# A spectral layer and two MLPs on one core: token chunks of 504 or 500 in place of 512 and a last 384

## The chip, the core and the metric

The kernel runs on one core of a Trainium2 chip. The metric is device time in microseconds (us) from the first to the last instruction; lower is better. Engines are named as the profile names them: PE multiplies matrices (PEld is its weight load), DVE, ACT and POOL work elementwise, SP issues the DMAs. TensorE has two clock levels, 1.2 and 2.4 GHz; the profile shows the granted one.

## What is computed

Cut to what matters, with B x S = 2 x 3008 = 6016 tokens of 256 features and 2048 hidden units:

```python
X = rfft(x, axis=1)
Y = soft_threshold(X @ (w_r + 1j * w_i) + b, 0.01)
y = irfft(Y, n=3008).reshape(6016, 256)
h = y @ w_in1
y = (h * sigmoid(h)) @ w_out1
h = y @ w_in2
out = np.maximum(0.01 * h, h) @ w_out2
```

All of it is in float32. The two MLPs (layer 1 and layer 2) are the part that the change touches.

## The kernel before, in words

**Numbers in two halves.** To keep float32 accuracy from single-pass matmuls, every operand is a rounded high part and a rest, the low part. A product is three matmuls: low weights by high data, high weights by low data, high by high (`product`, L574). ACT casts the high parts (`high`, L567), and DVE or POOL subtracts to get the low parts (`lower`, L530).

**Chunks and pairs.** Tokens run along the free axis. `CHUNKS` (L27) cuts the 6016 tokens into eleven chunks of 512 and a last one of 384. Each layer goes over the 12 chunks, and in each chunk over 8 pairs of hidden tiles of 128. A pair makes two tiles ph with `first` (L499): 6 matmuls for each, 12 in all, over the n tokens of the chunk. Then come the activation (`activate`, L509) and the products of the second matrix.

**Three modes of the second matrix** (L496). It has two hidden tiles by two output tiles in a pair.
- "plain" (layer 1, chunks 0 and 1): four products over n tokens, 12 matmuls.
- "blocks" (chunks of 512): the chunk is split into two halves of 256 tokens, and seven products over half a chunk do the work of eight, 21 matmuls. The seven need sums of hidden blocks: `t1` on POOL, `t23` and `t4` on DVE, into the tile u of six blocks. Their results stand in four accumulators and are put together at the end of the chunk in `finish` (L607).
- "tail" (the chunk of 384): four products over 384 tokens, 12 matmuls, with no `t1` and no `t4`, two accumulators, and a `finish` of two copies (L620 on ACT, L621 on DVE).

**The order of the work** is written out by hand: instructions stand on each engine as the last loop (from L656) issues them. One turn of the loop handles three pairs at once. The newest (`pr`) does `first` and `activate`; the one before (`one`) makes its sums, casts and subtractions; the one before that (`two`) multiplies. Between them `make_next` issues steps for the coming chunk:
- in layer 1 `inverse` (L402), which multiplies the inverse transform into px and splits it into the ring of x tiles (xhi by ACT, xlo by DVE, L416 and L417);
- in layer 2 `load_x2` and, in the turn of the last pair of a chunk, twice `split_x2` (L428), which casts xhi on ACT and subtracts xlo on POOL (L432).

In that last turn the two `split_x2` stand before and behind `pr.t1()` on POOL. The first `first` of the next chunk needs both.

**The ring** (L398) holds 3 x 512 tokens; a token's place is its number modulo 1536. `inverse` makes 376 or 188 tokens at a time, and cuts them only where the ring wraps.

**Weights.** In the last chunk of layer 1 the weights of layer 2 are made: `next_in` (L485 on ACT, L486 on DVE) from its second pair on, `sums_w2` on POOL (L462) and `split_w` (L468 on ACT, L469 on DVE) from its fourth and fifth pair on, and these go on into the first pairs of layer 2.

The functions that the change touches, with the line numbers of the profile:

Of the kernel before, what the change touches and what calls it, by code (L numbers as in the profile page):

```python
# [71 lines left out]
def spectral_mlp_kernel(ctx, tc, x, w_r, w_i, b_r, b_i, w_in1, w_out1, w_in2, w_out2, da, ea, dm, out):  # L72
# [325 lines left out]
    ring = [big.tile([128, 2, RING], F32R, name=f"x{p}") for p in parts]  # L398
    at = lambda t: t % RING
    accs, x2f, late = {}, {}, {}  # L400

    def inverse(h, c):  # L402
# [25 lines left out]
    def split_x2(c, h):  # L428
        t0, n = CHUNKS[c]
        hi, lo = (r[:, h, at(t0):at(t0) + n] for r in ring)  # L430
        nc.scalar.copy(hi, x2f[c][h])
        nc.gpsimd.tensor_tensor(out=lo, in0=x2f[c][h], in1=hi.bitcast(F32), op=ALU.subtract)  # L432
# [55 lines left out]
    class Pair:  # L488
# [51 lines left out]
        def t1(self):  # L540
            if self.mode == "blocks":
                blk = lambda k: self.u[:, k * 256:(k + 1) * 256]
                nc.gpsimd.tensor_tensor(out=blk(1), in0=blk(0), in1=blk(2), op=ALU.subtract)  # L543

        def t23(self):
            u, b2, n = self.u, self.ph[1], self.n
            if self.mode == "blocks":
                v = u.rearrange("p (j n) -> p j n", n=256)
                b22 = b2[:, :256].rearrange("p (j n) -> p j n", j=1).to_broadcast([128, 2, 256])
                nc.vector.tensor_tensor(out=v[:, 3:5], in0=b22, in1=v[:, 0:2], op=ALU.subtract)  # L550
            else:
                nc.vector.tensor_tensor(out=u[:, n:2 * n], in0=b2, in1=u[:, :n], op=ALU.subtract)

        def t4(self):
            u, b2 = self.u, self.ph[1]
            if self.mode == "blocks":
                nc.vector.tensor_tensor(out=u[:, 1280:], in0=u[:, 1024:1280], in1=b2[:, 256:], op=ALU.subtract)  # L557

        def parts(self, which):
            n = self.n  # L560
            if which == "1":
                return self.h1, self.l1, self.ph[1]
            if self.mode == "blocks":
                return (self.ha, self.la, self.u[:, 256:768]) if which == "a" else (self.hb, self.lb, self.u[:, 768:])
            return (self.ha[:, :n], self.la[:, :n], self.u[:, :n]) if which == "a" else (self.hb[:, :n], self.lb[:, :n], self.u[:, n:2 * n])
# [13 lines left out]
        def acc(self, i):  # L579
            key = self.layer, self.c, i  # L580
            if key not in accs:
                accs[key] = ps_a[i // 2].tile([128, 512], F32, tag="acc", name="acc")
            return accs[key]

        def products(self, which):
            if self.mode == "plain":
                s = "ab".index(which)
                f = 2 * self.p + s
                hi, lo = ((self.ha, self.la), (self.hb[:, :512], self.lb[:, :512]))[s]
# [6 lines left out]
            blk = lambda a, k: a[:, k * 256:(k + 1) * 256]  # L596
            if self.mode == "blocks":
# [4 lines left out]
            else:  # L602
                for i, w, b, e in {"1": [(0, A12, True, False)], "a": [(0, A11, False, True), (1, S1, True, False)],
                                   "b": [(1, A22, False, True)]}[which]:
                    self.product(self.acc(i)[:, :self.n], wh[w], wl[w], hi, lo, b, e)

        def finish(self, part):  # L607
            if self.p != NF // 2 - 1:
                return
            key, n = (self.layer, self.c), self.n  # L610
# [8 lines left out]
            if self.mode != "blocks":  # L619
                nc.scalar.copy(o[0], self.acc(0)[:, :n])  # L620
# [149 lines left out]
```

## Time and profile before

| what | value |
|---|---|
| median of 3 runs | 1210.31 us (1208.16 to 1210.81) |
| profiled execution, span (the only time it has) | 1212.1 us |
| PE busy | 1199.7 us, 99% |
| PEld busy | 1074.2 us, 89% |
| DVE, ACT, POOL busy | 843.5, 782.8, 567.2 us |
| mean granted clock of TensorE | 0.997 |

The profiled execution is one run of its own and is 1.8 us longer than the median of the others. Matmuls are pipelined, and their recorded lengths overlap: a 128x256 matmul is recorded with 0.28 us while the next one starts 0.12 us after it. So the price of a matmul is read as the distance from one start to the next, over many of them. In a timeline a row gives the start, the length, the engine, the line, and the operation with output and inputs; "x2" merges two neighbours, and brackets tell how long the engine was idle before it and what ended that.

### The profile page before, as it was taken

The page shows a single profiled execution, that of the slowest core. Times are in us where ns is not written, and L with a number is a line of the kernel's source. Part 1 is how long each engine was busy: PE and PEld are TensorE (multiplying, and loading weights), DVE is VectorE, ACT ScalarE, POOL GpSimd, SP SyncE. Part 2 cuts the span into 40 slices and gives each one's busy share as a digit, 9 for nine tenths or more (in the row PEclk, how much of TensorE's full clock was granted, in tenths as well). Part 3 has the DMA queues.
Part 4 walks back from the last instruction along what each step waited for, and adds up shares of the span by engine and source line. Part 5 has one row for each costly group of instructions (what it writes and reads, how often), then busy time and mean ns, then how long its engine had stood idle before and what let it go on. Part 6 is the DMA issues. An engine that isn't in the chain of part 4 may idle for free.

```text
span 1212.1 us, 20092 instructions
## 1 busy us (share of the span) xinstructions
PE 1199.7 (99%) x7346; PEld 1074.2 (89%) x7346; DVE 843.5 (70%) x1525; ACT 782.8 (65%) x1614; POOL 567.2 (47%) x606
## 2 busy tenths in 40 slices
PE   9899999999999999999999999999999999999998
PEld 9788888888999999989999988988888898888898
DVE  0588879768888988888888895555555455555543
ACT  3698977656666666666665776656656665665664
POOL 0233525544444444544545575555545455554532
PEclk9899999999999999999999999999999999999999
DMA  9344444001111111101100110111011011001000
GB/s 212 100 122 127 147 124 137 24 14 48 51 36 59 58 40 49 57 26 55 45 26 19 35 32 1 35 36 35 2 36 36 1 36 35 29 8 36 32 1 31
DMA packets 35883, 61.62 MB, mean 51 GB/s; under 512 B 3908, under 2 KB 15784, under 8 KB 35784
## 3 DMA queue, kind: packets, MB, share of 16 engines
q1 hardware_dynamic: 35784, 60.33, 16.3%
q8 instruction: 58, 0.95, 0.3%
q14 instruction: 41, 0.34, 0.1%
HBM read 41.70 MB, written 18.61 MB: 50 GB/s over the span
## 4 chain that ended last, share of the span: by engine, by line
PE 92%; DMA 2%; DVE 2%; ACT 1%; POOL 1%; issue 1%; SPq 0%; DVEq 0%; ACTq 0%; POOLq 0%
PE ph L506 43%; PE acc L576 39%; PE pz L310 5%; PE py L329 3%; DMA xt<-in_x_dram 2%; PE px L409 2%; PE pb L352 1%; DVE wm L128 1%; DVE zl L320 0%; ACT wm L125 0%; PE pa L255 0%; SPq L237 0%; DVE py L337 0%; POOL xlo L432 0%; DVE alo L302 0%
## 5 line engine op out<-in xcount | busy, mean ns | idle before, releaser
L531 POOL TENSOR_TENSOR la<-u,ha 128x512 fp32r<-128x512 f32 (+1 forms) x176 | 232.7, 1322 | 246.8 <-ACT ha L569 246.0
L531 DVE TENSOR_TENSOR lb<-u,hb 128x768 fp32r<-128x768 f32 (+1 forms) x176 | 178.2, 1013 | 220.7 <-ACT hb L569 219.0
L506 PE MATMUL ph<-xhi,winlo 128*128 128x512 f32 (+1 forms) x768 | 240.3, 394 | 0.5 <-DVE la L531 0.5
L506 PE MATMUL ph<-xlo,winhi 128*128 128x512 f32 (+1 forms) x768 | 239.1, 391 | 1.2 <-POOL xlo L432 1.2
L506 PE MATMUL ph<-xhi,winhi 128*128 128x512 f32 (+1 forms) x768 | 237.6, 391 | 0.0
L525 ACT ACTIVATE u<-ph 128x512 f32<-128x512 f32 (+1 forms) x192 | 113.7, 592 | 142.7 <-PE ph L506 142.6
L506 PEld LDWEIGHTS ph<-xlo,winhi 128*128 128x128 f32 x768 | 144.0, 188 | 36.3 <-POOL xlo L432 5.5
L506 PEld LDWEIGHTS ph<-xhi,winhi 128*128 128x128 f32 x768 | 143.8, 188 | 30.8
L543 POOL TENSOR_TENSOR u<-u 128x256 f32<-128x256 f32 x160 | 125.8, 786 | 65.2 <-DVE u L526 58.6
L569 ACT CAST hb<-u 128x768 fp32r<-128x768 f32 (+1 forms) x176 | 140.3, 797 | 9.4 <-DVE u L557 4.9
L576 PE MATMUL acc<-lb,whi 128*128 128x256 f32 (+1 forms) x496 | 141.1, 284 | 0.0
L576 PE MATMUL acc<-hb,whi 128*128 128x256 f32 (+1 forms) x496 | 139.6, 281 | 0.0
L576 PE MATMUL acc<-hb,wlo 128*128 128x256 f32 (+1 forms) x496 | 139.5, 281 | 0.0
L528 ACT ACTIVATE ph<-ph 128x512 f32<-128x512 f32 (+1 forms) x96 | 55.1, 574 | 113.2 <-PE ph L506 113.2
L506 PEld LDWEIGHTS ph<-xhi,winlo 128*128 128x128 f32 x768 | 120.5, 189 | 3.9 <-DVE la L531 1.0
L526 DVE SCALAR_TENSOR_TENSOR ph<-u,ph 128x512 f32<-128x512 f32 (+1 forms) x112 | 76.5, 683 | 65.1 <-ACT u L525 65.0
L569 ACT CAST ha<-u 128x512 fp32r<-128x512 f32 (+1 forms) x176 | 109.7, 623 | 14.7 <-POOL u L543 14.7
L531 DVE TENSOR_TENSOR l<-ph,h 128x512 fp32r<-128x512 f32 (+1 forms) x176 | 117.2, 666 | 0.0
L550 DVE TENSOR_TENSOR u<-ph,u 128x512 f32<-128x512 f32 x160 | 109.0, 681 | 6.3 <-POOL u L543 6.3
L569 ACT CAST h<-ph 128x512 fp32r<-128x512 f32 (+1 forms) x176 | 102.2, 581 | 2.6 <-DVE ph L526 1.5
L576 PE MATMUL acc<-ha,whi 128*128 128x256 f32 (+1 forms) x352 | 102.2, 290 | 0.0
L576 PE MATMUL acc<-la,whi 128*128 128x256 f32 (+1 forms) x352 | 100.9, 287 | 0.0
(123 smaller groups left out, 2675.8 us busy)
## 6 DMA issues: line engine op xcount, KB each, us to landing
wraw<-in_moe_w_in_dram SPq DMA_DIRECT2D x32, 256.0 KB
wraw<-in_moe_w_out_dram SPq DMA_DIRECT2D x32, 256.0 KB
scr<-bo SPq DMA_DIRECT2D x48, 128.0 KB
scr<-x2o SPq DMA_DIRECT2D x22, 256.0 KB
x2i<-scr SPq DMA_DIRECT2D x22, 256.0 KB
out_dram<-x2o SPq DMA_DIRECT2D x22, 256.0 KB
dmr<-in_dm_dram SPq DMA_DIRECT2D x34, 160.0 KB
bt<-scr SPq DMA_DIRECT2D x14, 384.0 KB
```

Of the source, the lines that this page charges most:

```text
L310: nc.tensor.matmul(pz, lhsT=u[:, h, :], rhs=v[:, h].rearrange("p g e -> p (g e)"), start=(n == 0), stop=(n == len(terms) - 1))
L329: nc.tensor.matmul(py, lhsT=u, rhs=v, start=(n == 0), stop=(n == len(terms)))
L409: nc.tensor.matmul(px[:, s * PAIR:(s + 1) * PAIR], lhsT=bt[:, s, h * 128:(h + 1) * 128], rhs=ea_sb, start=True, stop=True, skip_group_chec ...
L506: nc.tensor.matmul(ph, lhsT=u[:, h, f * 128:(f + 1) * 128], rhs=v[:, h, :], start=(i == 0), stop=(i == len(terms) - 1))
L525: nc.scalar.activation(out=th, in_=ph, func=ACTF.Tanh)
L526: nc.vector.scalar_tensor_tensor(out=out, in0=th, scalar=1.0, in1=ph, op0=ALU.add, op1=ALU.mult)
L528: nc.scalar.activation(out=out, in_=ph, func=ACTF.Prelu, alpha=0.01)
L531: eng.tensor_tensor(out=lo, in0=src, in1=hi.bitcast(F32), op=ALU.subtract)
L543: nc.gpsimd.tensor_tensor(out=blk(1), in0=blk(0), in1=blk(2), op=ALU.subtract)
L550: nc.vector.tensor_tensor(out=v[:, 3:5], in0=b22, in1=v[:, 0:2], op=ALU.subtract)
L569: nc.scalar.copy(hi, src)
L576: nc.tensor.matmul(dst, lhsT=u, rhs=v, start=(begin and self.p == 0 and i == 0), stop=(end and self.p == NF // 2 - 1 and i == 2), skip_gro ...
```

## The change

Twelve chunks of 504 (the first four) or 500 tokens take the place of eleven of 512 and one of 384. Every chunk but the two plain ones now runs in mode "blocks"; the halves are 252 or 250 tokens. The mode "tail" is gone. The ring has three slots of 504 tokens, and chunk c lies in slot c modulo 3, so that `inverse` cuts its tokens at every border of chunks.

```diff
-CHUNKS = [(t0, min(512, TOK - t0)) for t0 in range(0, TOK, 512)]
+SIZES = [504] * 4 + [500] * 8
+CHUNKS = [(sum(SIZES[:c]), n) for c, n in enumerate(SIZES)]
 NG = 4
-RING = 3 * 512
+SLOT = max(SIZES)
...
+    def place(c, a=0, b=None):
+        s = c % 3 * SLOT
+        return slice(s + a, s + (CHUNKS[c][1] if b is None else b))
...
-        cut = min(t1, t0 + RING - at(t0))
-        for a, b in ((t0, cut), (cut, t1)):
+        for k, (s0, size) in enumerate(CHUNKS):
+            a, b = max(t0, s0), min(t1, s0 + size)
             if a < b:
-                hi, lo = (r[:, h, at(a):at(a) + b - a] for r in ring)
+                hi, lo = (r[:, h, place(k, a - s0, b - s0)] for r in ring)
...
-            self.mode = "plain" if layer == 1 and c < 2 else "blocks" if self.n == 512 else "tail"
+            self.mode = "plain" if layer == 1 and c < 2 else "blocks"
...
+        def blk(self, a, k, m=1):
+            nb = self.n // 2
+            return a[:, k * nb:(k + m) * nb]
...
         def t1(self):
-            if self.mode == "blocks":
-                blk = lambda k: self.u[:, k * 256:(k + 1) * 256]
-                nc.gpsimd.tensor_tensor(out=blk(1), in0=blk(0), in1=blk(2), op=ALU.subtract)
+            blk = lambda k: self.blk(self.u, k)
+            nc.gpsimd.tensor_tensor(out=blk(1), in0=blk(0), in1=blk(2), op=ALU.subtract)
...
-            if self.mode == "blocks":
-                for i, k, w, j in {"1": [(0, 0, S4, 0), (0, 1, A12, 1)],
-                                   "a": [(1, 0, S1, 0), (2, 0, A11, 1)],
-                                   "b": [(1, 1, S3, 0), (2, 1, S2, 1), (3, 0, A22, 2)]}[which]:
-                    self.product(blk(self.acc(i), k), wh[w], wl[w], blk(hi, j), blk(lo, j), k == 0)
-            else:
-                for i, w, b, e in {"1": [(0, A12, True, False)], "a": [(0, A11, False, True), (1, S1, True, False)],
-                                   "b": [(1, A22, False, True)]}[which]:
-                    self.product(self.acc(i)[:, :self.n], wh[w], wl[w], hi, lo, b, e)
+            blk = self.blk
+            for i, k, w, j in {"1": [(0, 0, S4, 0), (0, 1, A12, 1)],
+                               "a": [(1, 0, S1, 0), (2, 0, A11, 1)],
+                               "b": [(1, 1, S3, 0), (2, 1, S2, 1), (3, 0, A22, 2)]}[which]:
+                self.product(blk(self.acc(i), k), wh[w], wl[w], blk(hi, j), blk(lo, j), k == 0)
```

The other lines of the diff put n or n/2 in the place of 512 and 256 in slices and views. Line numbers of the changed kernel are a few larger or smaller.

How the order moves is shown at three places. First PE, where the products of the last pair of a chunk stand (wlo and whi are the weights, h, ha, hb the high parts and l, la, lb the low parts of the three operands). Before, at the end of the last chunk of layer 2:

```order
L576 MATMUL acc<-h_14016,wlo 128x384
L576 MATMUL acc<-l_14017,whi 128x384
L576 MATMUL acc<-h_14016,whi 128x384
L576 MATMUL acc<-ha,wlo 128x384
L576 MATMUL acc<-la,whi 128x384
L576 MATMUL acc<-ha,whi 128x384
```

And of the change, the same place:

```order
L575 MATMUL acc<-h_14208,wlo 128x250
L575 MATMUL acc<-l_14209,whi 128x250
L575 MATMUL acc<-h_14208,whi 128x250
L575 MATMUL acc<-h_14208,wlo 128x250
L575 MATMUL acc<-l_14209,whi 128x250
L575 MATMUL acc<-h_14208,whi 128x250
```

Each operand now has one product for each of its blocks (two of h, two of ha, three of hb), where before there was one of h, two of ha and one of hb. In all PE has 5558 rows in place of 5414: 144 matmuls more.

Second POOL where layer 1 ends and layer 2 begins (wsum are sums of weights, la and u those of the last pairs of layer 1, xlo that of the first chunk of layer 2). Before:

```order
L462 TENSOR_TENSOR wsum<-m_3686,wsum 128x128
L531 TENSOR_TENSOR la<-u,ha 128x384
L432 TENSOR_TENSOR xlo<-x2i,xhi 128x512 x2
L462 TENSOR_TENSOR wsum<-m_3686 128x128 x2
L462 TENSOR_TENSOR wsum<-wsum,m_3686 128x128
```

Of the change:

```order
L466 TENSOR_TENSOR wsum<-m_3694,wsum 128x128
L539 TENSOR_TENSOR la<-u,ha 128x500
L436 TENSOR_TENSOR xlo<-x2i,xhi 128x504
L550 TENSOR_TENSOR u<-u 128x250
L436 TENSOR_TENSOR xlo<-x2i,xhi 128x504
```

The `t1` of the last pair of layer 1 now stands between the two subtractions that layer 2 begins with.

Third DVE at the end of the program. Before:

```order
L552 TENSOR_TENSOR u<-ph,u 128x384
L531 TENSOR_TENSOR l_14017<-ph,h_14016 128x384
L531 TENSOR_TENSOR lb<-u,hb 128x384
L621 COPY x2o<-acc 128x384
L765 UNCONDITIONAL_BRANCH
```

Of the change:

```order
L559 TENSOR_TENSOR u<-u,ph 128x250
L539 TENSOR_TENSOR lb<-u,hb 128x750
L624 TENSOR_TENSOR x2o<-x2o,acc 128x250 x2
L625 TENSOR_TENSOR x2o<-x2o,acc 128x250
L626 TENSOR_TENSOR u<-u,acc 128x250
L627 TENSOR_TENSOR x2o<-x2o,acc 128x250
```

One copy has become five operations, and two on POOL (L628, L629) stand behind them.

## Rows read from the trace of the kernel before

**Rows 1.** The page: busy time of the engines, and the granted clock by slices.

```profile
PE 1199.7 (99%) x7346; PEld 1074.2 (89%) x7346; DVE 843.5 (70%) x1525; ACT 782.8 (65%) x1614; POOL 567.2 (47%) x606
...
PEclk9899999999999999999999999999999999999999
```

**Rows 2.** The page: the chain that ended last, by engine and by line.

```profile
PE 92%; DMA 2%; DVE 2%; ACT 1%; POOL 1%; issue 1%; SPq 0%; DVEq 0%; ACTq 0%; POOLq 0%
PE ph L506 43%; PE acc L576 39%; PE pz L310 5%; PE py L329 3%; DMA xt<-in_x_dram 2%; PE px L409 2%; PE pb L352 1%; DVE wm L128 1%; DVE zl L320 0%; ACT wm L125 0%; PE pa L255 0%; SPq L237 0%; DVE py L337 0%; POOL xlo L432 0%; DVE alo L302 0%
```

**Rows 3.** Timeline of PE, one pair of layer 2 in blocks of 256.

```profile
900.57 0.28 PE L576 MATMUL acc<-h,wlo 128*128 128x256 f32 x1
...
901.28 0.63 PE L506 MATMUL ph<-xhi,winlo 128*128 128x512 f32 x2
...
902.68 0.28 PE L576 MATMUL acc<-ha,wlo 128*128 128x256 f32 x1
...
904.46 0.63 PE L506 MATMUL ph<-xhi,winlo 128*128 128x512 f32 x2
```

**Rows 4.** Timeline of PE, one pair of the last chunk, mode tail.

```profile
1186.04 0.34 PE L576 MATMUL acc<-ha,wlo 128*128 128x384 f32 x1
...
1190.22 0.34 PE L576 MATMUL acc<-ha,wlo 128*128 128x384 f32 x1
```

**Rows 5.** Timeline of PE, the narrowest matmuls of the kernel, and the next one.

```profile
165.93 1.92 PE L409 MATMUL px<-ea_sb,bt 96*128 96x94 f32 x16
167.63 0.71 PE L310 MATMUL pz<-wmlo,ahi 128*128 128x512 f32 x2
```

**Rows 6.** Timeline, the end of the program, mode tail.

```profile
1208.17 1.47 SPq L638 DMA_DIRECT2D out_dram<-x2o  x2
1208.35 0.34 PE L576 MATMUL acc<-hb,whi 128*128 128x384 f32 x1
1208.72 0.56 DVE L621 COPY x2o<-acc 128x384 f32<-128x384 f32 x1 [2.51 <-PE acc L576]
```

**Rows 7.** Timeline, the finish of the chunk before, mode blocks.

```profile
1178.40 0.28 PE L576 MATMUL acc<-hb,whi 128*128 128x256 f32 x1
...
1178.93 0.60 ACT L626 COPY x2o<-acc 128x512 f32<-128x512 f32 x1
...
1179.12 0.28 PE L576 MATMUL acc<-hb,whi 128*128 128x256 f32 x1
...
1179.56 0.75 DVE L630 TENSOR_TENSOR x2o<-x2o,acc 128x256 f32<-128x256 f32 x2 [0.41 <-ACT x2o L626]
...
1181.80 1.31 POOL L635 TENSOR_TENSOR x2o<-x2o,u 128x512 f32<-128x512 f32 x1
```

**Rows 8.** Timeline of PE where layer 1 ends and layer 2 begins.

```profile
697.32 0.51 PE L506 MATMUL ph<-xhi,winhi 128*128 128x384 f32 x2
...
701.27 0.41 PE L506 MATMUL ph<-xlo,winhi 128*128 128x512 f32 x1
702.86 0.50 PE L506 MATMUL ph<-xlo,winhi 128*128 128x512 f32 x1 [1.18 <-POOL xlo L432]
```

**Rows 9.** Timeline of POOL there.

```profile
698.66 1.02 POOL L531 TENSOR_TENSOR la<-u,ha 128x384 fp32r<-128x384 f32 x1 [0.68 <-ACT ha L569]
699.64 3.17 POOL L432 TENSOR_TENSOR xlo<-x2i,xhi 128x512 fp32r<-128x512 f32 x2
```

**Rows 10.** Timeline of DVE there: the first operation of three turns, and rows between.

```profile
690.30 0.54 DVE L552 TENSOR_TENSOR u<-ph,u 128x384 f32<-128x384 f32 x1
...
694.41 0.68 DVE L486 TENSOR_TENSOR winlo<-m,winhi 128x512 fp32r<-128x512 f32 x1
695.01 0.54 DVE L552 TENSOR_TENSOR u<-ph,u 128x384 f32<-128x384 f32 x1
...
699.89 1.80 DVE L486 TENSOR_TENSOR winlo<-m,winhi 128x512 fp32r<-128x512 f32 x1
701.61 0.55 DVE L552 TENSOR_TENSOR u<-ph,u 128x384 f32<-128x384 f32 x1
...
702.54 0.54 DVE L526 SCALAR_TENSOR_TENSOR u<-u,ph 128x384 f32<-128x384 f32 x1
```

**Rows 11.** Timeline of layer 1 in mode blocks: DVE and POOL operations on wider tiles.

```profile
652.88 0.41 DVE L557 TENSOR_TENSOR u<-u,ph 128x256 f32<-128x256 f32 x1
653.21 0.68 DVE L526 SCALAR_TENSOR_TENSOR u<-u,ph 128x512 f32<-128x512 f32 x1
653.96 0.74 POOL L543 TENSOR_TENSOR u<-u 128x256 f32<-128x256 f32 x1
```

**Rows 12.** Waits of PE from 690 to 725 us: us in total, times, longest.

```profile
PE acc L576 <- ACT x2o L620: 0.6, 1, 0.6
```

**Rows 13.** Waits of PE from 170 to 300 us, and a narrow split of x on DVE.

```profile
PE ph L506 <- DVE la L531: 0.5, 2, 0.3
...
644.37 0.34 DVE L417 TENSOR_TENSOR xlo<-px,xhi 128x188 fp32r<-128x188 f32 x1
```

More of the change, by code (lines that the diff above doesn't have):

```diff
@@ L397, in spectral_mlp_kernel @@
     m4 = pool("m4", 2, side="right", **near)
-    ring = [big.tile([128, 2, RING], F32R, name=f"x{p}") for p in parts]
-    at = lambda t: t % RING
+    ring = [big.tile([128, 2, 3 * SLOT], F32R, name=f"x{p}") for p in parts]
+    def place(c, a=0, b=None):
+        s = c % 3 * SLOT
+        return slice(s + a, s + (CHUNKS[c][1] if b is None else b))
     accs, x2f, late = {}, {}, {}
@@ L428, in split_x2 @@
     def split_x2(c, h):
-        t0, n = CHUNKS[c]
-        hi, lo = (r[:, h, at(t0):at(t0) + n] for r in ring)
+        hi, lo = (r[:, h, place(c)] for r in ring)
         nc.scalar.copy(hi, x2f[c][h])
@@ L495, in __init__ @@
             self.t0, self.n = CHUNKS[c]
-            self.mode = "plain" if layer == 1 and c < 2 else "blocks" if self.n == 512 else "tail"
+            self.mode = "plain" if layer == 1 and c < 2 else "blocks"
             self.ph = {}
         def first(self, s):
-            f, t0, n = 2 * self.p + s, self.t0, self.n
-            hi, lo = (r[:, :, at(t0):at(t0) + n] for r in ring)
+            f, n = 2 * self.p + s, self.n
+            hi, lo = (r[:, :, place(self.c)] for r in ring)
             self.ph[s] = ph = ps_h.tile([128, 512], F32, tag="h", name="ph")[:, :n]
@@ L533, in split_plain @@
         def split_plain(self):
-            for ph, hi, lo in ((self.ph[0], self.ha, self.la), (self.ph[1], self.hb[:, :512], self.lb[:, :512])):
+            for ph, hi, lo in ((self.ph[0], self.ha, self.la), (self.ph[1], self.hb[:, :self.n], self.lb[:, :self.n])):
                 nc.scalar.copy(hi, ph)
@@ L609, in finish @@
                 return
-            key, n = (self.layer, self.c), self.n
+            key, n, nb = (self.layer, self.c), self.n, self.n // 2
             if part == 0:
@@ L619, in finish @@
             if self.mode != "blocks":
-                nc.scalar.copy(o[0], self.acc(0)[:, :n])
-                nc.vector.tensor_copy(o[1], self.acc(1)[:, :n])
+                nc.scalar.copy(o[0], self.acc(0))
+                nc.vector.tensor_copy(o[1], self.acc(1))
             else:
-                half = lambda a, k: a[:, k * 256:(k + 1) * 256]
+                half = self.blk
                 both = lambda a: a.rearrange("p (k n) -> p k n", k=2)
-                twice = lambda a: a.rearrange("p (k n) -> p k n", k=1).to_broadcast([128, 2, 256])
+                twice = lambda a: a.rearrange("p (k n) -> p k n", k=1).to_broadcast([128, 2, nb])
                 nc.scalar.copy(both(o[1]), twice(half(self.acc(1), 1)))
-                u = stage.tile([128, 256], F32, tag="wc", bufs=4, name="u")
+                u = stage.tile([128, 256], F32, tag="wc", bufs=4, name="u")[:, :nb]
                 nc.scalar.copy(u, half(self.acc(2), 0))
@@ L701, in spectral_mlp_kernel @@
             make_next()
-            pr.t1()
+            if pr.mode == "blocks":
+                pr.t1()
             if pr.p == NF // 2 - 1:
```

39 lines of the change are left out of this document (15 added, 24 removed).

## Prediction

> **What bounds the kernel now.** I read the page's busy times and clock first. PE is busy for 1199.7 of 1212.1 us and its clock is granted in full in nearly every slice [rows 1]. The chain that ended last says the same: 92% of it is PE, and 82% are the two matmul lines of the MLPs, `first` and the products [rows 2]. So the first question is how much PE time the change takes away, and the second is what happens at the few places where PE stops. For both the timelines count, not the busy time, since recorded matmuls overlap.
>
> **The price of a matmul**, from starts. In a pair of layer 2 the six 512-wide matmuls from 901.28 to 902.68 us are 233.3 ns apart. The six 256-wide ones from 900.57 to 901.28 and the fifteen from 902.68 to 904.46 take 0.71 + 1.78 = 2.49 us, 118.6 ns each [rows 3]. A pair of the last chunk has 24 matmuls of 384 in 1190.22 - 1186.04 = 4.18 us, 174.2 ns each [rows 4]. Between 384 and 256 a column costs (174.2 - 118.6) / 128 = 0.434 ns, between 512 and 384 it costs 0.462 ns.
>
> **The change, part by part.**
>
> *PE, `first`.* There are 12 chunks before and after, so 12 x 8 x 12 = 1152 matmuls in each layer, and the sum of their columns stays. At 0.462 ns a column 504 costs 229.6 ns and 500 costs 227.8. After: 768 x 229.6 + 1536 x 227.8 = 526.2 us. Before: 2112 x 233.3 + 192 x 174.2 = 526.2 us. The term is 0.
>
> *PE, products.* Before, 20 chunks in blocks have 20 x 8 x 21 = 3360 matmuls at 118.6 ns, 398.5 us, and the two chunks in mode tail have 192 at 174.2 ns, 33.4 us: 431.9 us. After, there are 22 x 168 = 3696: six chunks of half-width 252 with 1008, and sixteen of 250 with 2688. No row has these widths. Above, the nearest is 256 at 118.6 ns; below, the only narrower matmul is px, 94 wide: sixteen records from 165.93 to 167.63 us, 106 ns apart [rows 5]. So the price lies between 106 and 118.6 ns. I take the line through 256 and 384, as 256 is by far the nearer: 116.9 and 116.0 ns. That makes 117.8 + 311.8 = 429.6 us, -2.3 us. If a matmul cost in proportion to its columns, it would be 116.8 and 115.8 ns, -3.0 us; if the price stuck at 118.6 ns, 3696 x 118.6 = 438.3 us, +6.4 us.
>
> *PE, plain.* 192 products of 504 in place of 512, 3.7 ns less each: -0.7 us. PE in all: -3.0 us, with ends at -3.7 and +5.7.
>
> *The end of the program.* In mode tail the last matmul starts at 1208.35 and ends at 1208.69; one DVE copy ends at 1209.28, 0.6 us later, and the rest to 1212.1 is its DMA [rows 6]. In mode blocks the finish is a chain: ACT copies, DVE adds five times, POOL adds twice. The chunk before shows it. Its last matmul ends at 1179.12 + 0.28 = 1179.40 and POOL's last add at 1181.80 + 1.31 = 1183.11, 3.7 us later [rows 7]. There the second ACT copy was held up: its matmul ended at 1178.68 and it began at 1178.93 behind another copy. At the end ACT is idle, so I take off 0.2 us, and 0.1 us for narrower tiles: 3.4 us in place of 0.6, +2.8 us. In the chunk before this hid behind the next chunk's matmuls; at the end that cover is gone. Ends: +2.4 (DVE starting earlier still) and +3.5 (a last DMA of 500 columns in place of 384, and PE waiting for the longer lb of the last pair).
>
> *Where layer 1 ends.* Before, PE stood 1.18 us for the second xlo [rows 8] and 0.6 us for the copy of an accumulator by ACT [rows 12]. The copy is one of mode tail's; blocks have other accumulators free there, so this wait goes. The first one changes. Before, POOL did both xlo back to back, 699.64 to 702.81 [rows 9]. Now `t1` of the last pair stands between them. It needs that pair's first activation on DVE, and DVE is behind: the `first` ended at about 697.67 [rows 8], the DVE operation stood at 702.54 to 703.08 [rows 10], 5.4 us later, since the splits of layer 2's weights fill DVE (its turns take 4.71 and 6.60 us where PE's take 4.18). In blocks PE's turn grows by 1.0 us to 5.2, and DVE's by about 1.4 as an estimate: four operations of 0.54 become about 0.67, lb grows by twice as much, t4 adds 0.4 [rows 10, 11]. So DVE is no less behind. The second xlo is then ready 5.4 + 0.4 (t4, now ahead of it) + 0.74 (t1, rows 11) + 1.6 (half of 3.17) = 8.1 us after `first` ended. PE wants it after 21 products, 6 matmuls and 3 more: 2.4 + 1.4 + 0.7 = 4.5 us. That is a wait of 3.6 us. While POOL waits for `t1`, though, DVE is not slowed by it: its 128x512 split took 1.80 us beside POOL's xlo and 0.68 without [rows 10]. I take off 1.0: 2.6 us in place of 1.2 + 0.6, +0.8 us. Ends: -1.8 (no wait is left) and +3.0.
>
> *More cuts.* `inverse` cut 3 of its 18 groups at the wrap of the ring, now all 11 groups that hold a border of chunks: 8 more, for two halves of features, 16 more ACT casts and 16 more DVE subtractions. Two narrow ones cost more than a wide one only by the fixed part, less than the 0.34 us of the 188-wide one [rows 13], so under 5 us on DVE, spread over 500 us. DVE's queue is what stands behind them, and PE waits for it in the plain chunks alone, 0.5 us in two waits [rows 13]: +0.3 us, between 0 and +1.0. Later, the two turns between a pair's splitting and its products hide them; without that cover the bound would be 5 us.
>
> **Sum:** -3.0 + 2.8 + 0.8 + 0.3 = +0.9 us on the span of 1212.1, so 1213.0 for a profiled run. The median of the runs is 1.8 us lower than that execution, and I carry the difference over: 1210.3 + 0.9 = **1211.2 us**. A measurement of this kernel can tell about 0.2% from no change, 2.4 us, so below 1207.9 counts as faster and above 1212.7 as slower. The forecast is no change: a small gain on PE is paid back at the two places where mode tail was short.
>
> **Rivals.**
>
> *The weight load sets the pace of a narrow matmul.* The products grow by 144 weight loads, and if the 118.6 ns at 256 were a load's and not a stream's, they would get no cheaper: +6.4 in place of -2.3, 1211.2 + 8.7 = 1219.9 us. For it: PEld is busy for 89% of the span [rows 1], and px pays 106 ns for 94 columns, so something other than columns sets a least price. Against it: that least price is 10 ns below the 116.0 that I ask of 250 columns. It decides from the point where a load takes over 116 ns. The Trainium skill has a rule that speaks for this rival (TensorE: Matmul & The Clock Gate, section LDWEIGHTS): a weight load's time goes by its 128 columns alone, whatever the matmul streams. Its figure is an estimate of 107 ns here, and px's 106 ns agrees; by that figure 250 columns would still be above the least price, though not by much. Chance 0.08.
>
> *The last turn of layer 1 gets worse than I reckon* (the rival on the slower side that I fear more). If POOL's `t1` waits the full time, the second xlo comes 3.6 us late, and the DVE work queued behind, the finish of a chunk in blocks on top of layer 2's weight splits, makes PE wait for accumulators for 2 us more: +3.8 in place of +0.8, 1214.2 us. It decides once DVE is more than about 6 us behind PE; it was 5.4 behind [rows 8, 10]. The Trainium skill (SBUF - State Buffer, section on two separate sides) says that DVE and POOL share a port pair by an exclusive lock, so that one stands still while the other works. The 1.80 us beside 0.68 agrees; by that rule three POOL operations in a row with DVE's splits are done one after the other. Chance 0.20.
>
> *Faster.* The longer turns let DVE catch up, the wait at the end of layer 1 goes away (-1.8), the finish at the end is at its short end (+2.4), cuts cost nothing, and products are cheap in proportion: -3.7 - 1.8 + 2.4 = -3.1, 1207.2 us. For it: PE's turn of 5.2 us is longer, and DVE had idle time in the first turns of that chunk. Against it: `t1` stands in the way on POOL. Chance 0.17.
>
> **How the numbers follow.** The forecast with its own range of 1208.5 to 1213.0 has 0.50; the three rivals 0.08, 0.20 and 0.17; 0.05 is left for prices that no row shows, such as reads that no longer start at multiples of 1 KB, half on each side. Faster takes the third rival but for a part that ends near 1207.9, and the remainder: 0.18. Slower takes the first two and a part of the forecast: 0.30. No change: 0.52. The range for 8 in 10 leaves out the first rival and the ends of the others: 1207.0 to 1216.0.
>
> **What would show it.** Products of 250 at 116.0 ns and of 252 at 116.9 from start to start; `first` at 228 to 230. From the end of the last matmul to POOL's last add 3.4 us. At the start of layer 2 one PE wait for xlo of 2 to 3 us and no wait for x2o. No PE wait over 0.5 us in the chunks of layer 1 after the plain ones. It is wrong if products stay at 118 ns or above, if the wait at the start of layer 2 is gone or over 4 us, or if new waits show inside the chunks.

## The result, and the profile after

| | before | after |
|---|---|---|
| median of the four runs compared | 1209.89 us | 1217.59 us (1217.08 to 1218.36) |
| ratio | | 1.0072 (1.0059 to 1.0085) |
| profiled execution, span | 1212.1 us | 1215.7 us |
| first `first` of the MLPs to the last matmul | 1035.97 us | 1042.13 us |
| last matmul's start to the end | 3.74 us | 6.51 us |

The changed kernel is slower by 0.72%, 7.7 us, outside the predicted range. The two profiled executions differ by 3.6 us only since that of before began its MLPs 5.3 us later, in work that the change doesn't touch; from there on they are 6.16 + 2.77 = 8.93 us apart.

The page of after, answering to [rows 1, 2]: PE is as busy as before, but one slice in the middle shows clock 8, and the chain that ended last has 4% DVE.

```profile
PE 1199.4 (99%) x7490; PEld 1076.7 (89%) x7490; DVE 854.1 (70%) x1565; ACT 788.0 (65%) x1634; POOL 558.4 (46%) x626
...
PEclk9999999999999999999999989999999999999999
...
PE 90%; DVE 4%; DMA 2%; ACT 1%; POOL 1%; issue 1%; SPq 0%; POOLq 0%; DVEq 0%; ACTq 0%
```

That slice is the start of layer 2. The waits of PE of after, from 640 to 760 us (total, times, longest), answering to [rows 12]:

```profile
PE ph L510 <- POOL xlo L436: 3.9, 2, 2.2
PE ph L510 <- ACT xhi L435: 0.8, 1, 0.8
PE acc L575 <- DVE l L539: 0.3, 2, 0.2
```

PE there, answering to [rows 8] (brackets: idle before, and what ended it); the first row stands right behind the first `first` of the last pair of layer 1. PE waits for xhi and for both xlo, where before it waited for the second xlo alone:

```profile
690.68 0.28 PE L575 MATMUL acc<-h,wlo 128*128 128x250 f32 x1
...
695.93 1.01 PE L510 MATMUL ph<-xhi,winlo 128*128 128x504 f32 x2 [0.79 <-ACT xhi L435]
698.67 0.49 PE L510 MATMUL ph<-xlo,winhi 128*128 128x504 f32 x1 [1.73 <-POOL xlo L436]
701.32 0.79 PE L510 MATMUL ph<-xlo,winhi 128*128 128x504 f32 x1 [2.15 <-POOL xlo L436]
701.90 1.04 PE L510 MATMUL ph<-xhi,winhi 128*128 128x504 f32 x2
...
706.48 0.28 PE L575 MATMUL acc<-ha,wlo 128*128 128x250 f32 x1
```

Behind the waits the matmuls are slow: from 701.90 to 706.48 eight of 504 columns and six of 250 take 4.58 us, where eight of 229 ns and six of 117 make 2.53. By stretches (PE, PEld, DVE, ACT, POOL busy, then PEclk), PE was busy for a third of 695 to 700 us, and then the granted clock fell to 0.50, the lower level, 1.2 GHz:

```profile
690.00:695.00 5.00, 4.81 (x31) 4.12 (x29) 5.00 (x9) 3.55 (x9) 3.77 (x5) 1.00 0.02 5
695.00:700.00 5.00, 1.63 (x5) 0.56 (x3) 5.00 (x9) 3.88 (x10) 4.90 (x6) 0.96 0.00 0
700.00:705.00 5.00, 3.68 (x12) 3.24 (x13) 5.00 (x8) 2.03 (x4) 4.92 (x7) 0.50 0.00 0
705.00:710.00 5.00, 5.00 (x30) 4.45 (x29) 2.56 (x7) 3.33 (x9) 2.38 (x5) 0.86 0.01 2
```

DVE is busy all the time there. Its timeline in after, answering to [rows 10]: the first operation of four turns and rows between.

```profile
683.29 0.66 DVE L556 TENSOR_TENSOR u<-ph,u 128x500 f32<-128x500 f32 x1
...
689.85 0.67 DVE L556 TENSOR_TENSOR u<-ph,u 128x500 f32<-128x500 f32 x1
...
696.40 0.66 DVE L556 TENSOR_TENSOR u<-ph,u 128x500 f32<-128x500 f32 x1
...
697.89 0.66 DVE L530 SCALAR_TENSOR_TENSOR u<-u,ph 128x500 f32<-128x500 f32 x1
...
700.08 2.07 DVE L473 TENSOR_TENSOR wlo<-wsum,whi 128x256 fp32r<-128x256 f32 x2
...
703.99 0.67 DVE L556 TENSOR_TENSOR u<-ph,u 128x500 f32<-128x500 f32 x1
```

Its turns take 6.6, 6.6 and 7.6 us, PE's 5.2. POOL in after, answering to [rows 9]. t1 of the pair before the last starts only when DVE has made its u, and four sums of weights, la and both xlo stand behind it without a gap:

```profile
692.09 0.72 POOL L550 TENSOR_TENSOR u<-u 128x250 f32<-128x250 f32 x1 [1.23 <-DVE u L530]
692.77 1.76 POOL L466 TENSOR_TENSOR wsum<-m 128x128 f32<-128x128 f32 x2
...
695.89 1.52 POOL L539 TENSOR_TENSOR la<-u,ha 128x500 fp32r<-128x500 f32 x1
697.36 1.25 POOL L436 TENSOR_TENSOR xlo<-x2i,xhi 128x504 fp32r<-128x504 f32 x1
698.63 0.72 POOL L550 TENSOR_TENSOR u<-u 128x250 f32<-128x250 f32 x1
699.32 1.95 POOL L436 TENSOR_TENSOR xlo<-x2i,xhi 128x504 fp32r<-128x504 f32 x1
```

The end of the program in after, answering to [rows 6, 7]:

```profile
1209.18 0.28 PE L575 MATMUL acc<-hb,whi 128*128 128x250 f32 x1
...
1211.58 1.15 POOL L629 TENSOR_TENSOR x2o<-x2o,u 128x500 f32<-128x500 f32 x1
```

To compare whole chunks, here is the distance from the first matmul of a chunk to that of the next (every 96th `first` of the timeline; us). "Steady" are later chunks of layer 2 (with the new sizes, the narrower ones).

| kernel | last of layer 1 | first of layer 2 | second | steady |
|---|---|---|---|---|
| before | 34.2 | 44.2 | 42.5 | 42.5 |
| after | 43.0 | 49.3 | 41.7 | 41.5 to 41.9 |
| e1_late | 41.6 | 47.7 | 44.6 | 41.4 to 41.9 |
| e5_spread | 41.6 | 51.8 | 41.5 | 41.4 to 41.9 |
| e8_xearly | 43.1 | 48.2 | 41.5 | 41.2 to 41.6 |
| e9_spread2 | 41.6 | 47.2 | 44.4 | 41.5 to 41.9 |
| e11_tail1 | 43.0 | 42.0 | 41.8 | 41.4 to 41.9 |
| e13_best500 | 41.6 | 42.2 | 42.3 | 41.2 to 41.6 |
| e15_bxe | 34.2 | 43.7 | 42.3 | 42.3 |
| e17_spread3 | 41.6 | 44.8 | 47.4 | 41.4 to 41.9 |

After loses 43.0 + 49.3 - 41.6 - 41.7 = 9.0 us at the border of the layers; 41.6 is the last chunk of layer 1 where the weights are out of its way (e1_late), 41.7 the second chunk of layer 2. Before loses 44.2 - 41.7 = 2.5: its first chunk of layer 2 holds two pairs of products of the narrow last chunk, at 12 x 174.2 ns = 2.09 us in place of 21 x 118.6 ns = 2.49 us each, so undisturbed it would take 0.8 us less than the later 42.5.

### The profile page after: what moved, and what is told of

The parts are those of the page before. It is cut to its first block, busy times and chain, and to the rows that moved or that the text cites. A ratio compares the mean times of both kernels' runs of the same rounds, so it can differ in the third digit from the quotient of the medians.

```text
span 1215.7 us, 20504 instructions
## 1 busy us (share of the span) xinstructions
PE 1199.4 (99%) x7490; PEld 1076.7 (89%) x7490; DVE 854.1 (70%) x1565; ACT 788.0 (65%) x1634; POOL 558.4 (46%) x626
## 4 chain that ended last, share of the span: by engine, by line
PE 90%; DVE 4%; DMA 2%; ACT 1%; POOL 1%; issue 1%; SPq 0%; POOLq 0%; DVEq 0%; ACTq 0%
PE ph L510 42%; PE acc L575 37%; PE pz L311 5%; PE py L330 3%; PE px L414 2%; DMA xt<-in_x_dram 2%; PE pb L353 1%; DVE wlo L473 1%; PE pa L256 1%; DVE wm L129 1%; DVE zl L321 0%; SPq L238 0%; ACT wm L126 0%; DVE lb L539 0%; DVE py L338 0%
## 5 line engine op out<-in xcount | busy, mean ns | idle before, releaser
L539 DVE TENSOR_TENSOR lb<-u,hb 128x750 fp32r<-128x750 f32 (+1 forms) x176 | 178.6, 1015 | 221.7 <-ACT hb L568 220.1
L539 POOL TENSOR_TENSOR la<-u,ha 128x500 fp32r<-128x500 f32 (+1 forms) x176 | 208.5, 1184 | 241.2 <-ACT ha L568 240.3
L510 PE MATMUL ph<-xlo,winhi 128*128 128x500 f32 (+1 forms) x768 | 240.5, 392 | 3.9 <-POOL xlo L436 3.9
L510 PE MATMUL ph<-xhi,winlo 128*128 128x500 f32 (+1 forms) x768 | 240.9, 394 | 1.9 <-DVE la L539 1.1
L510 PE MATMUL ph<-xhi,winhi 128*128 128x500 f32 (+1 forms) x768 | 238.3, 391 | 0.0
L550 POOL TENSOR_TENSOR u<-u 128x250 f32<-128x250 f32 (+1 forms) x176 | 135.6, 770 | 87.5 <-DVE u L530 73.1
L568 ACT CAST hb<-u 128x750 fp32r<-128x750 f32 (+1 forms) x176 | 143.4, 815 | 13.0 <-DVE u L559 12.9
L575 PE MATMUL acc<-lb,whi 128*128 128x250 f32 (+1 forms) x528 | 147.7, 280 | 0.0
L575 PE MATMUL acc<-hb,wlo 128*128 128x250 f32 (+1 forms) x528 | 147.4, 279 | 0.0
L575 PE MATMUL acc<-hb,whi 128*128 128x250 f32 (+1 forms) x528 | 147.4, 279 | 0.0
L539 DVE TENSOR_TENSOR l<-ph,h 128x500 fp32r<-128x500 f32 (+1 forms) x176 | 117.3, 666 | 0.0
```

The lines of the kernel that those rows point to most:

```text
L510: nc.tensor.matmul(ph, lhsT=u[:, h, f * 128:(f + 1) * 128], rhs=v[:, h, :], start=(i == 0), stop=(i == len(terms) - 1))
L568: nc.scalar.copy(hi, src)
L575: nc.tensor.matmul(dst, lhsT=u, rhs=v, start=(begin and self.p == 0 and i == 0), stop=(end and self.p == NF // 2 - 1 and i == 2), skip_gro ...
```

## Experiments

The theory after the result: blocks give DVE more work than a turn holds while it also splits the weights of layer 2, its lag makes POOL and then PE late at the border (rest of the loss: 250 columns are dear, and the end). Each ratio is to the kernel before, beside which the runs were made. The medians of before there lie between 1208.56 and 1209.89 us, so microseconds of runs made at different times compare to about 1 us only.

**Each part alone.** e1_late (weights of layer 2 four turns later) and e2_w496 (sizes):

```diff
-            if 0 <= i - tail - 1 < k:
-                next_in(i - tail - 1)
-            if 0 <= i - tail - 3 < k:
-                sums_w2(i - tail - 3)
+            if 0 <= i - tail - 5 < k:
+                next_in(i - tail - 5)
+            if 0 <= i - tail - 7 < k:
+                sums_w2(i - tail - 7)
```

```diff
-SIZES = [504] * 4 + [500] * 8
+SIZES = [504] * 8 + [496] * 4
```

> The changed kernel, with the making of layer 2's weights begun four turns later, so that it falls into layer 2. Theory (the splits of these weights put DVE behind in the last chunk of layer 1, and PE's waits at the start of layer 2 follow from that): the waits there, 5.0 us by the view of waits and about 2.6 us of lowered clock behind them, fall under 1 us together, and the time to about 1210 us. Rival (the first block sum on POOL between the two subtractions of x, and the longer operations of a chunk in blocks, cause them by themselves): a wait of 3 to 5 us stays, 1213 to 1215 us.

> The changed kernel with eight chunks of 504 and four of 496, so halves of 252 and 248. In the changed kernel a product of 250 columns took 117.1 ns from start to start, and one of 252 took 116.1. Theory (250 columns are 1000 bytes and no longer a multiple of 16, and that costs 1 to 2 ns): 248 costs about 115 ns, 252 stays at 116.1; products take 3.9 us less, 1213.7 us. Rival (from some 252 columns down the weight load sets the pace): 248 costs 117 ns or more, and the time stays within 1 us of the changed kernel.

e1: 1218.16 us, ratio 1.0082 (1.0068 to 1.0096), neither forecast. The border is free, but PE waits later, in the first two chunks of layer 2 (waits of PE of e1_late, 640 to 760 us):

```profile
PE acc L575 <- DVE l L539: 5.1, 3, 1.9
PE ph L510 <- POOL xlo L436: 2.3, 2, 1.6
```

So the place of the loss goes with the weights, and not its size. e2: 1214.09 us, 1.0042 (1.0028 to 1.0055), 3.5 below after, as expected. 248 columns cost 114.7 ns from start to start, 252 116.1; 250 cost 117.05 in after, more than 252.

e3_cuts (the kernel before, with x cut at every border of chunks) and e4_tail2 (after, with the last chunk of layer 2 by four full-width products and the short finish):

```diff
-        cut = min(t1, t0 + RING - at(t0))
-        for a, b in ((t0, cut), (cut, t1)):
+        for s0, size in CHUNKS:
+            a, b = max(t0, s0), min(t1, s0 + size)
```

```diff
-            self.mode = "plain" if layer == 1 and c < 2 else "blocks"
+            self.mode = "plain" if layer == 1 and c < 2 else "tail" if layer == 2 and c == len(CHUNKS) - 1 else "blocks"
...
```

The other lines bring back what mode tail did, `t1` and `t4` left out included.

> The kernel before, with the one addition that the inverse transform's tokens are cut at every border of chunks of 512. Theory of the prediction: within 1 us of the kernel before, as PE waits for DVE in the plain chunks alone. Rival (the narrow splits hold PSUM buffers and DVE longer, and cost PE up to half a us each): 2 to 3 us slower.

> The changed kernel with the last chunk of layer 2 (500 tokens) as four full-width products for a pair in place of seven of half the width. Theory (the finish of a chunk in blocks, a chain over ACT, DVE and POOL, costs 2.8 us at the end): from the end of the last matmul to the end of the program 3.4 us in place of 6.2, against 2.2 us more on PE (96 matmuls of 228 ns in place of 168 of 117), so about 1217 us. Rival (the end is longer because the last DMA is): 6 us stay, 1219 to 1220 us.

e3: 1209.69 us, 1.0004 (0.9996 to 1.0013): the cuts cost nothing that can be measured. e4: 1217.34 us, 1.0068 (1.0054 to 1.0081). The last matmul starts at 1210.48 and the span ends at 1214.5, 4.1 us in place of 6.5, so the finish makes 2.4 of the 2.8 us by which the end grew. Full-width products take about 2 us more (estimated from 96 matmuls of 228 ns and 168 of 117), and leaving the finish out pays nothing net. Both terms came out about as reckoned.

**Where the last chunk of layer 1 isn't in blocks.** e11_tail1 is e4's edit, for that chunk alone:

```diff
-            self.mode = "plain" if layer == 1 and c < 2 else "blocks"
+            self.mode = "plain" if layer == 1 and c < 2 else "tail" if layer == 1 and c == len(CHUNKS) - 1 else "blocks"
...
```

> The changed kernel with the last chunk of layer 1 alone by four full-width products (12 matmuls of 500 a pair, as mode tail had). PE does 12 x 226.9 - 21 x 117.05 = 265 ns more in a pair, 2.1 us in all. Theory (blocks' wider DVE operations in that chunk are what makes DVE late): the loss at the boundary falls from 9.4 us to before's 2.7 or less, 1217.5 - 6.7 + 2.1 = 1213 us, 1212 to 1214. Rival (the loss comes from the order of t1 and xlo or from the longer turn, not from DVE's load): 1217 us or more.

1210.30 us, 1.0012 (1.0003 to 1.0021), better than the theory asked. PE does 2.1 us more there, and still 7.3 us are won: the border had cost about 9.4. No wait of PE is left from 640 to 760 us, and the clock stays (stretches of e11_tail1):

```profile
695.00:700.00 5.00, 5.00 (x23) 4.14 (x23) 5.00 (x8) 3.76 (x10) 4.92 (x7) 1.00 0.01 2
700.00:705.00 5.00, 5.00 (x23) 4.13 (x22) 4.91 (x9) 3.86 (x10) 4.92 (x7) 1.00 0.02 5
```

e11 leaves out the `t1` of that chunk too, so by itself it doesn't tell DVE's load from the place of `t1` on POOL. e1_late and e5_spread (below) do: `t1` stays where it was, only the weights move, and PE has no wait over 0.2 us at the border. DVE's lag goes the same way. Measured as in the prediction, from the start of the matmul behind the last pair's first `first` to the end of DVE's operation on that result, it is 698.55 - 690.68 = 7.9 us in after. In e11 (the weights, but no blocks) it is 694.19 - 691.87 = 2.3, in e1_late (blocks, but the weights later) 693.31 - 691.27 = 2.0; e11 first:

```profile
691.87 0.40 PE L585 MATMUL acc<-h,wlo 128*128 128x500 f32 x1
...
693.53 0.66 DVE L530 SCALAR_TENSOR_TENSOR u<-u,ph 128x500 f32<-128x500 f32 x1
```

```profile
691.27 0.28 PE L575 MATMUL acc<-h,wlo 128*128 128x250 f32 x1
...
692.64 0.67 DVE L530 SCALAR_TENSOR_TENSOR u<-u,ph 128x500 f32<-128x500 f32 x1
```

So the loss at the border takes both, blocks and weights in one chunk.

e12_w192 goes the other way: all chunks in blocks with the sizes of before.

```diff
-SIZES = [504] * 4 + [500] * 8
+SIZES = [512] * 11 + [384]
```

> The changed kernel with the sizes of before, eleven chunks of 512 and one of 384, the 384 too by blocks, of 192 columns. If a least price near that of px (106 ns) holds, 336 products take 35.6 us in place of 192 x 174.2 = 33.4; by columns alone (0.434 ns each from 118.6 at 256) 90.8 ns, 30.5 us. PE's turn there is then 12 x 174.2 + 21 x 91 to 106 = 4.0 to 4.3 us, shorter than the changed kernel's 5.2, while DVE gets t4 and a wider lb: by the theory of DVE's lag the loss at the boundary is at least the changed kernel's 9.4 us, so 1209 - 2.7 + 9.4 + 2.5 (end) + 2.2 or - 2.9: 1215 to 1221 us. If the loss at the boundary came from the new sizes and not from the mode: under 1213.

1220.87 us, 1.0094 (1.0079 to 1.0110). The first two chunk distances at the border are 37.4 and 49.0 us, with 4.9 us of waits (waits of e12_w192, 640 to 760 us):

```profile
PE ph L510 <- POOL xlo L436: 3.7, 2, 2.1
PE ph L510 <- ACT xhi L435: 0.8, 1, 0.8
PE acc L575 <- DVE l L539: 0.4, 1, 0.4
```

So it is the mode of that chunk that brings the loss, not its size. 192 columns cost 110.0 ns, where the line through 256 and 384 gives 90.8: from 244 columns (113.6 ns in e16_s508, below) to 192 the price falls by 3.6 ns only.

**The order of x and weights.** e8_xearly splits x earlier, in the turns of the sixth and seventh pair of a chunk. e5, e9 and e17 spread the weights by tables of turns:

```diff
-            return [lambda: load_x2(c)] + [None] * 4 + [lambda h=h: split_x2(c, h) for h in range(2)]
+            return [lambda: load_x2(c)] + [None] * 2 + [lambda h=h: split_x2(c, h) for h in range(2)]
```

```diff
-            if 0 <= i - tail - 1 < k:
-                next_in(i - tail - 1)
-            if 0 <= i - tail - 3 < k:
-                sums_w2(i - tail - 3)
+            if i - tail in (at_in := [1, 2, 3, 5, 8, 10, 12, 14]):
+                next_in(at_in.index(i - tail))
+            if i - tail in (at_out := [3, 5, 8, 9, 10, 12, 13, 14]):
+                sums_w2(at_out.index(i - tail))
```

> The changed kernel with both split_x2 two turns earlier (in the turns of the sixth and seventh pair of a chunk in place of twice in that of the eighth). Theory of the prediction (POOL's second xlo is late since t1 and the last la stand before it): all waits for xlo go, about 5 us with their share of the clock: 1211 to 1213. Theory of DVE's lag (DVE is 7 us behind PE there, and xlo is only the first thing that PE misses): the wait passes on to what DVE makes next, l or lb of the last pairs of layer 1, and the time falls by less than 3 us: 1215 to 1217.

> The changed kernel; only the turns in which layer 2's weights are made differ: the eight next_in in turns 1, 2, 3, 5, 8, 10, 12, 14 after the last chunk of layer 1 begins (before 1 to 8), the eight sums_w2 in turns 3, 5, 8, 9, 10, 12, 13, 14 (before 3 to 10), so that no turn but two has both splits and turn 7, where POOL splits x for layer 2, has neither sums nor next_in. Theory (the turns of layer 1's last chunk hold more DVE and POOL work than PE's 5.2 us, and only their crowding makes DVE late): the waits for xhi and xlo at the start of layer 2 and the low clock behind them go from 9.4 us to under 3, and no new waits come: 1210.5 to 1212.5 us. Rival (the sum of that work does not fit anywhere, as when it was moved four turns later): the waits come back in layer 2's first chunks, 1216 us or more.

> e5_spread with a mended plan: there next_in of the last pair stood in the turn just before its use, behind 7 us of DVE work, and PE waited 5.5 us for it. Now next_in in turns 1, 2, 3, 6, 8, 10, 12, 13 and sums_w2 in turns 3, 4, 6, 9, 10, 11, 13, 14, with at least two turns between making and use, and DVE's turn 9, which holds the finish of a chunk, left free. Theory (crowding alone): boundary under 3 us, no wait over 1.5 us in layer 2's first chunks, 1210.5 to 1212.5 us. Rival (DVE and POOL slow each other so much that the work fits nowhere): 1215 us or more, waits for l or xlo of 5 us and more in sum between 690 and 750.

> e5_spread with the last two next_in in turns 11 and 12 in place of 12 and 14; all else as there. Theory (it is what stands in the turn of the two xlo that counts): the 5.5 us wait for winlo of e5 goes and nothing else changes, boundary wait still 0.2 us, 1212 to 1213.5 us. Rival (the work only moves): 1215 or more, with a new wait of 2 us or more between 700 and 760.

e8: 1214.42 us, 1.0053 (1.0041 to 1.0065), between the forecasts, and the trace decides. The waits for xlo are gone, and as the theory of DVE's lag had it, PE waits for l, and for the copy of an accumulator (waits of e8_xearly, 640 to 760 us):

```profile
PE acc L575 <- DVE l L539: 3.3, 3, 1.1
PE acc L575 <- ACT x2o L609: 2.0, 1, 2.0
```

The border still takes 43.1 + 48.2 us, 1.0 less than after. The rest of the gain is elsewhere: every later chunk is 0.2 to 0.3 us shorter, 2.5 us over eleven. There PE ran just behind xlo at every chunk's start, before too. PE in the kernel before, and in e15_bxe below, at such a start (the second row is the one on xlo):

```profile
787.51 0.63 PE L506 MATMUL ph<-xhi,winlo 128*128 128x512 f32 x2
787.98 0.84 PE L506 MATMUL ph<-xlo,winhi 128*128 128x512 f32 x2
788.65 0.63 PE L506 MATMUL ph<-xhi,winhi 128*128 128x512 f32 x2
```

```profile
781.15 0.63 PE L506 MATMUL ph<-xhi,winlo 128*128 128x512 f32 x2
781.61 0.63 PE L506 MATMUL ph<-xlo,winhi 128*128 128x512 f32 x2
782.08 0.63 PE L506 MATMUL ph<-xhi,winhi 128*128 128x512 f32 x2
```

In both the middle row has two matmuls; 0.67 us to the next row in the first, 0.47 in the second. No list of waits shows this, since each lasts 0.1 us.

e5: 1218.57 us, 1.0084 (1.0071 to 1.0097). My plan was at fault: the border was cured, but a next_in stood one turn before its use, behind DVE's lag (waits of e5_spread, 640 to 760 us):

```profile
PE ph L510 <- DVE winlo L490: 5.4, 1, 5.4
PE acc L575 <- DVE l L539: 1.2, 2, 1.0
PE ph L510 <- POOL xlo L436: 0.2, 1, 0.2
```

e9: 1217.74 us, 1.0070 (1.0058 to 1.0083), the rival's forecast. Waits of 5.3 us for xlo, at the first and at the second chunk of layer 2. e17, e5 mended: 1218.16 us, 1.0073 (1.0060 to 1.0087), the rival's too: PE waited 0.2 us at the first border and 1.6 us for l in the chunk behind it, and the second chunk's start, 740 to 749 us, took the rest, with 2.6 us of waits for xlo and a clock of 0.74 and 0.58 (stretches of e17_spread3):

```profile
740.00:745.00 5.00, 2.21 (x5) 1.20 (x6) 3.83 (x5) 3.89 (x10) 5.00 (x5) 0.74 0.00 0
745.00:750.00 5.00, 5.00 (x21) 4.33 (x20) 2.94 (x6) 1.00 (x2) 1.35 (x2) 0.58 0.00 0
```

No placing of the weights that I tried helps by itself, while the last turn of a chunk holds both xlo: the waits only move, to l, to winlo or to the next chunk's xlo.

**Both together.** e13_best500 is e9's plan with e8's edit. e10_best2 has e2's sizes as well, e18_best3 the same with e17's plan, e6_spread496 is e5 with e2's sizes; e14_t1best is e11 with e8's edit and e2's sizes. The tables are the only new lines (e9, e13 and e10 above, e17 and e18 below):

```diff
+            if i - tail in (at_in := [1, 2, 3, 6, 8, 10, 12, 13]):
+            if i - tail in (at_out := [3, 4, 6, 9, 10, 11, 13, 14]):
...
+            if i - tail in (at_in := [1, 2, 3, 5, 8, 10, 11, 12]):
+            if i - tail in (at_out := [3, 5, 8, 9, 10, 12, 13, 14]):
```

> The changed kernel's sizes (504 and 500) with both moves of e10: layer 2's weights by the plan of e9 and split_x2 two turns earlier. If the two moves cure the boundary only together, and the 496 chunks are worth their own 3.4 us: 1205.2 + 3.4 = 1208.6, 1208 to 1209.5. If the 496 chunks are what cured it: 1213 or more.

> e9_spread2 with chunks of 504 (eight) and 496 (four), and with split_x2 two turns earlier as in e8_xearly. The gains add if their causes differ: e9_spread2 less 3.3 us for the products less 0.5 to 2 us for xlo, 1206 to 1208.5 us, below the kernel before. If splitting x earlier only meets the weights' splits: 1209 to 1212.

> e17 with chunks of 504 and 496 and split_x2 two turns earlier. If the plans are equally good once split_x2 is early: 1204.5 to 1206, as e10 (1205.24). If e9's plan is better for DVE: 1206 or more.

> As e5_spread, and with chunks of 504 (eight) and 496 (four). If the two causes are separate their gains add: e5_spread less 3 to 3.5 us, 1207 to 1209 us, below the kernel before. If the narrower chunk's gain came in part from a shorter boundary, less than 2 us below e5_spread.

> e11_tail1 (last chunk of layer 1 by four full-width products) with the sizes 504 and 496 and split_x2 two turns earlier, weights unspread as in the changed kernel. From the parts: 1210.3 - 3.4 (496) - 2.5 (0.21 to 0.24 us at the start of each chunk of layer 2) = 1204.4, 1203.5 to 1205.5. If moving split_x2 collides with the weights made in the sixth and seventh turn: 1206 or more.

e13: 1207.72 us, 0.9985 (0.9976 to 0.9994), 9.9 us below after. Its only wait in the list from 640 to 760 us is one of 0.5 us. Spreading alone won nothing and moving x alone 3.2 us (2.3 by the ratios); together they win about 10. e10: 1205.24 us, 0.9965 (0.9952 to 0.9978), below its forecast and faster than both kernels; e18: 1205.41, 0.9973 (0.9963 to 0.9983); e14: 1205.15, 0.9963 (0.9950 to 0.9975), within its forecast. All three are as fast, so the best version may be had with or without blocks at the border. e6: 1214.95, 1.0060 (1.0049 to 1.0072), 3.6 us below e5: the sizes' gain adds.

What splits of weights cost is read from two rows of the same two operations on DVE, in after (one turn ahead of the 2.07 us at 700.08) and in e13_best500, the first beside POOL's sums and the second while POOL is idle:

```profile
693.53 1.28 DVE L473 TENSOR_TENSOR wlo<-wsum,whi 128x256 fp32r<-128x256 f32 x2
```

```profile
688.04 0.75 DVE L473 TENSOR_TENSOR wlo<-wsum,whi 128x256 fp32r<-128x256 f32 x2
```

**Controls.** The same edits on the kernel before: e7_bspread has e5's plan, e15_bxe the earlier split_x2.

> The kernel before with the same turns for layer 2's weights as e5_spread. Theory: before, about 2.7 us were lost at the boundary, of which at most these can be had: 1207 to 1209 us. Rival (the spreading is a gain by itself of the size of e5_spread's, whatever the mode of the last chunk): 1204 us or less. If the work only moves: 1209 to 1212.

> The kernel before with split_x2 two turns earlier, nothing else. In its trace PE loses about 0.21 us at each of the 10 chunk starts of layer 2 after the first, 2.1 us, and 1.4 to 1.7 at the first: 1209.0 - 2.1 - 0 to 1.7 = 1205.2 to 1207. If the boundary there gets worse as DVE's lag passes to l: 1207 to 1209.

e7: 1212.38 us, 1.0035 (1.0022 to 1.0048), slower, with e5's fault (a wait of 4.0 us for winlo behind 732.57). e15: 1206.16 us, 0.9975 (0.9964 to 0.9986), with two waits left, 0.8 us for l and 0.5 for x2o. So most of what e10 and e14 win over the kernel before doesn't come from new sizes: e14, made at the same time as e15, is 1.0 us faster. And e13, of that time too, which has the sizes of the change and both remedies, is 1.6 us slower than e15: given the same remedy for x, the kernel before isn't beaten by chunks of 504 and 500.

**Width.** e16_s508 is e13 with `SIZES = [508] * 8 + [488] * 4`.

> e13_best500 with eight chunks of 508 and four of 488: products of 254 columns (1016 bytes a row, 8 over a multiple of 16) and 244 (976 bytes, a multiple of 16). Theory (a row length that is no multiple of 16 bytes costs about 1 to 1.5 ns): 254 above the line between 252 (116.1) and 256 (118.5), 118.3 ns or more, 244 at 113 to 114. Rival (the price goes by columns, 250 was dear for another reason): 254 at 117.3, 244 at 112.5 to 113.5.

1206.11 us, 0.9973 (0.9963 to 0.9983). 254 columns cost 118.5 ns, above the line between 252 and 256 (117.3), and 244 cost 113.6, as the theory of 16 bytes had it. But in after the 250 columns cost 115.7 to 115.8 ns in every third chunk and 117.3 to 118.1 in the others. Two groups of fifteen of after show it, 115.3 and 117.3 ns each:

```profile
900.13 0.28 PE L575 MATMUL acc<-ha,wlo 128*128 128x250 f32 x1
...
901.86 0.61 PE L510 MATMUL ph<-xhi,winlo 128*128 128x500 f32 x2
...
931.45 0.28 PE L575 MATMUL acc<-ha,wlo 128*128 128x250 f32 x1
...
933.21 0.62 PE L510 MATMUL ph<-xhi,winlo 128*128 128x500 f32 x2
```

Row length alone can't do that, so the cause stays open. The cheap chunks are those in slot 1 of the ring, which the products don't read; nothing was tried on it.

## Why the prediction was wrong

| term | predicted, us | measured, us |
|---|---|---|
| products | -2.3 | -0.1 (2688 x 117.05 ns + 1008 x 116.1 ns = 431.7 us; before 431.8) |
| `first`, plain | 0, -0.7 | -0.4, -1.0 (means from start to start) |
| end of the program | +2.8 | +2.8, and 0.2 for lb |
| where layer 1 ends | +0.8 | +6.5 (9.0 - 2.5) |
| more cuts | +0.3 | +0.5 in the trace, nothing measurable in e3 |

The measured terms make +8.5, near the 8.9 of the traces and somewhat over the 7.7 of the medians.

**The step that failed is the term "where layer 1 ends".** I named the right place, the right operation (xlo on POOL) and the right rival, "DVE is more than about 6 us behind", at 0.20 and 3.8 us. The sizes were wrong: +0.8 was forecast and +6.5 measured, and the sign that I had named, a wait over 4 us there, came with 3.9 us for xlo in two waits and 0.8 for xhi. There are three reasons.
- *DVE's lag was carried over, not added up.* I read 5.4 us before (703.08 - 697.67) and argued that DVE would be "no less behind". By the same measure after has 697.89 + 0.66 - 690.68 = 7.9 us, and for the three pairs ahead of it 2.7, 5.2 and 6.5. DVE's turns ahead of that were 6.6 us against PE's 5.2, so the lag grew by about 1.4 us in each. In e11 it was 2.3 us, and no wait was left.
- *I looked at the wrong `t1`.* That between the two xlo cost only its own 0.72 us. The `t1` one turn earlier waited for DVE, and POOL's sums, la and both xlo queued behind it. So the first xlo was late too; and xhi, since ACT had also stood for DVE (2.15 us before 691.45). e8 shows that xlo was only the first thing to be missed.
- *The clock.* After two waits close together the granted clock was 0.50 for 5 us, and the next matmuls took about 2.0 us more (4.58 us in place of 2.53). I had no term for it.

**Products.** I drew a line through 256 and 384 and took 116.0 ns for 250. 252 came in below that line (116.1 for 116.9), 250 above it (117.05), and the two errors left nothing of the gain. e2 shows that the gain was to be had, 3.5 us, with other widths. Both ends of that term held.

**The weight-load rival** is out: products of 250 and 252 columns didn't stay at 118.6 ns, and 192 columns went down to 110.0. The Trainium skill (TensorE: Matmul & The Clock Gate, section LDWEIGHTS) gives a load that goes by its own 128 columns; 110.0 ns at 192 and px's 106 ns at 94 agree that there is a floor, and that it lies below 116; no run shows that the load is what sets it. **DVE and POOL.** The two splits above took 1.28 us beside POOL's sums (after) and 0.75 with POOL idle (e13), and two of POOL's sums in after 1.76 us beside such splits and 0.88 where DVE had none (e11, at 682.84 us). The Trainium skill (SBUF - State Buffer, section on two separate sides) has the rule that the two share a port pair by an exclusive lock, among others when an operation of DVE with both inputs in SBUF meets one of POOL that reads SBUF; these rows agree. My working charged this to the last turn alone, and it came in every turn that had both.

## What to carry to other kernels

Where engines beside the bound work in turns, add their busy time up turn by turn and let the lag grow, over all turns that carry extra work; a lag read in one turn of the old kernel is no bound for the new one. A wait that disappears is only won when the next thing the slow engine makes isn't late as well: try the remedy for the consumer and for the producer together, since each alone can show little. And apply a remedy to the old kernel too, before the change is credited with it.

## What the runs showed of the hardware that I had not expected

- 250 columns cost more than 252 on average: 117.05 and 116.1 ns; 248 cost 114.7, 254 118.5, 244 113.6, 192 110.0. The price of 250 changes with a period of three chunks, between 115.7 and 118.1 ns.
- After two waits of 1.7 and 2.2 us with few matmuls between, the granted clock was 0.50 in the next 5 us; in before, after one wait of 1.18 us, it stayed at 1.00.
